# Rows of dV from TensorE products instead of DMA transposes, with other work moved between the stages of an attention segment

## The chip, the cores and the metric

The kernel runs on one NeuronCore of a Trainium2 chip. A core has five instruction streams: TensorE (PE: matrix products; PEld are its weight loads), VectorE (DVE), ScalarE (ACT), GpSimd (POOL) and SyncE (SP), which only starts DMAs. Products are written to PSUM[...]. The metric is the time of one execution on the device in microseconds; lower is better.

## The reference

A forward pass and all its gradients in one program. Segments of 32 tokens with 8 memory rows each run one after the other, since the memory of a segment is the first 8 output rows of the one before; the gradient runs through the same chain backwards. There are 64 segments, 32 heads of 128, a model width of 512 and a GLU of width 1792.

```python
for s in range(n_seg):
    xs = x[:, s * seg_len:(s + 1) * seg_len, :].copy()
    h = jnp.concatenate([mem, xs], axis=1)
    q = jnp.einsum('btd,dhe->bhte', h, Wq)
    k = jnp.einsum('btd,dhe->bhte', h, Wk)
    v = jnp.einsum('btd,dhe->bhte', h, Wv)
    scores = jnp.einsum('bhqe,bhke->bhqk', q, k) * scale
    scores = jnp.where(mask[None, None], scores, -1000000000.0)
    p = _softmax(scores, axis=-1)
    o = jnp.einsum('bhqk,bhke->bhqe', p, v)
    o = jnp.einsum('bhte,hed->btd', o, Wo)
    mem = o[:, :M, :].copy()
    outs.append(o[:, M:, :])
...
h = _layernorm(x, axis=-1) * (1 + ca) + sa
x = x + ga * _A_ref(h, A_mem0, A_Wq, A_Wk, A_Wv, A_Wo, A_seg_len)
h = _layernorm(x, axis=-1) * (1 + cb) + sb
x = x + gb * _B_ref(h, B_w_gate, B_w_up, B_w_down)
...
_out, _vjp = jax.vjp(_f, A_x, A_mem0, A_Wq, A_Wk, A_Wv, A_Wo, B_w_gate, B_w_up, B_w_down, c, w_mod)
```

The six parts `sa, ca, ga, sb, cb, gb` are the rows of `silu(c) @ w_mod`; the program returns the output and the eleven gradients.

## The kernel before, in words

The program has four stages: the forward segments (`phase2`), the GLU with its own gradients (`phase3`), the backward segments (`phase4`), and the weight gradients of the attention with the last layer-norm gradients (`phase5`, lines 1757 to 1831).

**Tiles.** The 32 heads of a segment are packed three to a group: eleven groups, each a 128-wide block in which three heads have 40 rows each. A tile of 1408 columns holds all eleven groups. Work on it is cut into three parts of four, four and three groups, each one PSUM bank (`pi` = 0, 1, 2). A product with the 32 rows of a segment as stationary operand uses only 32 columns of TensorE's array; four such products stand side by side by `tile_position`, and make one PSUM tile of 128 partitions that has to be summed over its four blocks afterwards ("fold"). `col_pass` (line 241) projects the rows of a segment this way, `col_mm` (209) and `pair_mm` (215) sum over heads; `pair_mm` uses two blocks for one half of the 512 columns and two for the other, so that its result is 256 wide.

**Tails.** The last 8 tokens of each segment do not depend on the chain (only the first 8 rows feed it), and neither do their gradients. Those rows are collected for four segments (`TailRows`, 1869) and multiplied once for all four, in pieces that `chunk()` puts where the caller wants them. In the same way `proj_b`/`turn_b` make the tail rows of q, k, v (forward) or of dO (backward) for the next four segments. `s4` is the place of a segment in its group of four; forward it runs 0 to 3, backward 3 to 0.

**A forward segment** (656 to 857): projections k, q, v (16 products for each half), whose rows `RA` are moved by VectorE and ScalarE; transposes of k and q (`turns`); scores and exponent (`st_exp`, 685), with one product of the identity and the mask added in PSUM for each of the eleven groups (691); a shift of v rows (`vshift`, 718); denominators (`den`, 697) in a tile of their own; weighted sums (`pv`); reciprocal and scaling (`ost`); transposes of the scaled rows (`ott`, 749); output projection in pairs; split of the result in a high and a low bf16 part (`split_pair`, 223), and the fold (`sum_pair`, 232), in which for each of four column blocks one product takes the high and one the low part. ScalarE copies the first 8 rows into the next segment's `hT` (841). The layer-norm of later tokens runs in between in steps `p1(j, 1..4)` (386 to 415): step k of a group stands in segment `s4` = k between the k and the q projection (766), the last before `ott(0)`. In segments 8 to 23 eight products of one part of `w_mod` stand between the denominators of parts 0 and 1 (805 to 810). PSUM: seven banks in one ring (`psp`) and one for tails.

**A backward segment** (1457 to 1610): the dO pass (`col_pass` with `WoT`, both halves moved as 512 columns to `RAd`, by VectorE and ScalarE), copies of `RAd` to `dOst` on GpSimd (1538), transposes of `RAd` (`turn`, 1384) moved to `dOT`, then `gv0` (dVT part 0), `dp` (11 products), `gv1`, `ds` (11), the sum over heads with `WvT`, transposes of dS (`dstt`), dKT and dQT (`grad_mm`, 1504), sums with `WkT`, the rest of `WvT`, and `WqT`, all in one tile `dh_ps`; `fold_split` (298) into four 256-wide pieces, one `chunk()` of 24 tail products while that goes on, `fold_sum` (313) with eight products, and the first 8 rows as `dyT` for the next segment. Behind the fold stand `proj_b` (16 products) in the segments `s4` = 3 and 2, and `turn_b` in 1.

The weight gradients need dV, dK and dQ with tokens in the partitions. `grad_out` (1513) has the transposed tile: after its last part SP starts a DMA transpose into `rows_x` (1517), and GpSimd later stores the rows (`row_stores`, 1519). Two wait for the next segment, behind its dO pass (`store_rows_x(1)`, 1541), the third until line 1567. GpSimd also starts the DMAs that bring the tail rows of dO into `dOst` (`dO_tails`, 1440). The tail gradients of a group come in by `get_da`/`get_db` in `s4` = 3 (1463, 1566). PSUM: six banks in a ring, one for `dh_ps`, one for tails.

`pin` (278) fixes each engine's order in both segment loops as it is written.

Of the kernel before, what the change touches and what calls it, by code (L numbers as in the profile page):

```python
# [40 lines left out]
class K:  # L41
# [146 lines left out]
    def mod_rest(self, psp, pool, k):  # L188
# [3 lines left out]
        st = {}  # L192
# [5 lines left out]
        def products():  # L198
# [4 lines left out]
            row = pool.tile([1, 128], F32, name="modrow", bufs=1)  # L203
            nc.scalar.activation(row[:], ps[0:1, :], AF.Copy)
            nc.gpsimd.dma_start(self.MODROW[:, sl], row[:])
# [26 lines left out]
    def sum_pair(self, psp, parts, name, tag):  # L232

        ft = psp.tile([128, self.cfg.DC, 32], F32, name=name + "_ft", tag=tag)
        for c in range(self.cfg.DC):
            for i in range(2):
                self.nc.tensor.matmul(ft[:, c, :], lhsT=parts[i][:, (c % 2) * 128:(c % 2) * 128 + 128],
                                      rhs=self.foldhalf[:, c // 2, :], start=(i == 0), stop=(i == 1))
        return ft

    def col_pass(self, psp, w, hf, lhs, rows, eng):

        E, DC = self.cfg.E, self.cfg.DC
        ps = psp.tile([128, 512], F32, name="pass_ps", tag="p")
        for c in range(DC):
            wc = w[:, c, :].rearrange("p (h e) -> p h e", e=E)
            for j in range(4):
                rhs = wc[:, 12 * hf + j:12 * hf + j + 10:3, :] if j < 3 else wc[:, 24 + 4 * hf:28 + 4 * hf, :]
# [4 lines left out]
        self.evac(eng, rows[:, 512 * hf:512 * hf + 512], ps[:])  # L253
# [44 lines left out]
    def fold_split(self, pool, ps, name, tags=""):  # L298

        nc = self.nc  # L300
        parts = []
        for h in range(2):
            sl = slice(256 * h, 256 * h + 256)
            hi = pool.tile([128, 256], BF16, name=name + "_hi", tag=f"{tags}hi{h}", bufs=1)
            nc.scalar.activation(hi[:], ps[:, sl], AF.Copy)  # L305
            parts.append(hi)
        for h in range(2):
            lo = pool.tile([128, 256], BF16, name=name + "_lo", tag=f"{tags}lo{h}", bufs=1)
            nc.vector.tensor_tensor(lo[:], ps[:, 256 * h:256 * h + 256], parts[h][:], op=ALU.subtract)  # L309
            parts.append(lo)  # L310
        return parts

    def fold_sum(self, psp, parts, name, tag):

        ft = psp.tile([128, self.cfg.DC, 32], F32, name=name + "_ft", tag=tag)
        for c in range(self.cfg.DC):
            for i in range(2):
                self.nc.tensor.matmul(ft[:, c, :], lhsT=parts[2 * i + c // 2][:, (c % 2) * 128:(c % 2) * 128 + 128],  # L318
                                      rhs=self.foldsel[:], start=(i == 0), stop=(i == 1))
# [109 lines left out]
    def phase2(self):  # L429
# [13 lines left out]
        with ExitStack() as ctx:  # L443
# [212 lines left out]
            for s in range(NS):  # L656
# [148 lines left out]
                if mod_r:  # L805
                    mod_r.pop()()
# [1213 lines left out]
```

## Time and profile before

| | |
|---|---|
| median of 4 runs | 3157.77 us (3151.9 to 3168.25) |
| profiled execution, its own time | 3168.25 us |
| its span, first to last instruction | 3166.4 us |
| mean granted TensorE clock | 0.985 |
| busy: TensorE / VectorE / GpSimd / ScalarE | 2985.0 / 1611.1 / 1481.0 / 1161.3 us |
| matmuls | 40069 |

The same by stretches of the span, in microseconds of busy time:

| stretch | us | TensorE | VectorE | ScalarE | GpSimd | DMA share |
|---|---|---|---|---|---|---|
| 50 to 1010, forward segments | 960 | 927.0 | 605.2 | 467.4 | 626.1 | 0.85 |
| 1010 to 1380, GLU | 370 | 327.9 | 263.0 | 132.0 | 199.0 | 0.87 |
| 1380 to 1580, its weight gradients | 200 | 190.4 | 56.3 | 41.5 | 35.5 | 0.76 |
| 1580 to 2590, backward segments | 1010 | 947.7 | 518.4 | 447.7 | 452.2 | 1.10 |
| 2590 to 3166, weight gradients | 576 | 568.9 | 144.0 | 64.0 | 158.7 | 0.67 |

A line of the profile names the source line, the engine, the operation, the tile written and those read, the shape, and either a start and a length (timeline) or sums. A wait line reads: who waited, for whom, microseconds in total, times, the longest. The end of a matmul is modelled[...], so the start of the next product is the better mark of what one costs.

### The profile page before, as it was taken

The numbers are of one execution on the slowest core, as the hardware profiler recorded it, in microseconds if no ns is written. First come the engines' busy times: TensorE is split into PE (matmuls) and PEld (weight loads), VectorE is DVE, ScalarE is ACT, GpSimd is POOL, SyncE is SP. The second block draws the span as 40 slices with busy tenths as digits, with TensorE's granted clock in tenths as the row PEclk, the third lists the DMA queues.
The fourth block names the chain that finished last, engine by engine and source line by source line (L and its number), as shares of the span: only waits on it lengthen the run. The fifth ranks groups of instructions, "written<-read, shape, count | busy, mean of one in ns | idle before, by whom it ended". The sixth has DMA issues, their size and how long they took to land.

```text
span 3166.4 us, 98844 instructions
## 1 busy us (share of the span) xinstructions
PE 2985.0 (94%) x40069; PEld 1730.3 (55%) x40069; DVE 1611.1 (51%) x3770; ACT 1161.3 (37%) x2829; POOL 1481.0 (47%) x2974
## 2 busy tenths in 40 slices
PE   5999999999998799989989999999899999999999
PEld 3666666666665444445555555555555554455454
DVE  4666666666655677742245555555455442222321
ACT  2444454445444333322144444444444430000111
POOL 3666666666665466531244444444344432233322
PEclk8999999999999899999999999999999999999999
DMA  8888788988888799898599999999999998666664
GB/s 292 206 206 210 193 207 201 202 200 210 200 205 238 174 218 211 215 273 263 195 227 263 267 254 259 264 276 266 238 256 261 242 286 298 212 196 215 196 231 145
DMA packets 936796, 726.14 MB, mean 229 GB/s; under 512 B 635954, under 2 KB 808530, under 8 KB 935956
## 3 DMA queue, kind: packets, MB, share of 16 engines
q1 hardware_dynamic: 806564, 509.77, 68.9%
q0 software_dynamic: 59120, 148.64, 13.8%
q10 hardware_dynamic: 70656, 61.41, 6.2%
q8 instruction: 316, 5.18, 0.7%
q14 instruction: 140, 1.15, 0.1%
HBM read 294.93 MB, written 276.35 MB: 180 GB/s over the span
## 4 chain that ended last, share of the span: by engine, by line
PE 44%; DMA 5%; issue 4%; ACT 2%; POOL 1%; DVE 1%; SPq 0%; ACTq 0%; POOLq 0%; DVEq 0%
PE dh_ps L212 10%; PE gps L1812 8%; PE pass_ps L249 4%; PE gps5o L1826 4%; PE g_ps L1509 3%; PE gps L1210 3%; PE dh_tps L212 2%; PE tps L1423 2%; PE dp_ps L1488 1%; DMA dOst<-RBd 1%; PE dp_ps L1496 1%; ACT RAd L61 1%; PE dh_ft L318 1%; POOL out_dram L1816 1%; PE turn_ps L1389 1%
## 5 line engine op out<-in xcount | busy, mean ns | idle before, releaser
L1812 PE MATMUL gps<-rows,hrows 128*128 128x512 bf16 (+2 forms) x2160 | 417.5, 355 | 0.0
L1812 PEld LDWEIGHTS <-hrows 128*128 128x128 bf16 x2160 | 211.1, 98 | 204.7
L249 PEld LDWEIGHTS <-hT 128*32 128x32 bf16 x6144 | 158.1, 97 | 161.5 <-issue 1.9
L1538 POOL COPY dOst<-RAd 96x512 bf16<-96x512 bf16 x128 | 78.3, 612 | 353.5 <-DVE RAd L63 342.2
L851 POOL TENSOR_TENSOR Pst<-Pst,rden 120x1408 bf16<-120x1408 bf16 x63 | 160.1, 2542 | 106.1 <-issue 77.9
L1816 POOL DMA_DIRECT2D out_dram<-ot x108 | 81.5, 755 | 253.9 <-DVE ot L63 138.5
L63 DVE CAST ot<-gps 128x512 bf16<-128x512 f32 (+3 forms) x76 | 48.1, 633 | 279.1 <-PE gps L1812 193.0
L61 ACT ACTIVATE ot<-gps 128x512 bf16<-128x512 f32 (+3 forms) x75 | 41.3, 551 | 353.9 <-PE gps L1812 211.2
L309 DVE TENSOR_TENSOR dh_lo<-dh_ps,dh_hi 128x256 bf16<-128x256 f32 x128 | 48.4, 420 | 240.3 <-ACT dh_hi L305 240.3
L212 PE MATMUL dh_ps<-WvT,dVT 128*32 128x512 bf16 x2048 | 136.3, 386 | 0.1
L1498 DVE SCALAR_TENSOR_TENSOR dS<-dp_ps,Pst_l 128x512 bf16<-128x512 f32 (+1 forms) x192 | 112.2, 640 | 44.0 <-PE dp_ps L1496 43.9
L249 PE MATMUL pass_ps<-Wv,hT 128*32 128x512 bf16 x2048 | 133.3, 380 | 0.0
L1826 PE MATMUL gps5o<-WoT,rows 128*128 128x512 bf16 x592 | 128.4, 379 | 1.1 <-DMA rows<-OSR 1.1
L249 PE MATMUL pass_ps<-WoT,dyT 128*32 128x512 bf16 x2048 | 123.6, 384 | 5.2 <-ACT dyT L1597 5.2
L220 PE MATMUL at_ps<-Wo,OT 128*32 128x256 bf16 x4096 | 125.3, 275 | 0.5 <-DVE OT L63 0.2
L249 PE MATMUL pass_ps<-Wk,hT 128*32 128x512 bf16 x2048 | 123.3, 383 | 1.5 <-ACT hT L841 1.1
L61 ACT ACTIVATE dVT<-g_ps 128x512 bf16<-128x512 f32 (+1 forms) x192 | 107.8, 561 | 44.7 <-PE g_ps L1509 28.6
L212 PE MATMUL dh_ps<-WkT,dKT 128*32 128x512 bf16 x2048 | 122.3, 380 | 0.0
L212 PE MATMUL dh_ps<-WqT,dQT 128*32 128x512 bf16 x2048 | 122.1, 379 | 0.0
L249 PE MATMUL pass_ps<-Wq,hT 128*32 128x512 bf16 x2048 | 121.6, 379 | 0.0
L63 DVE CAST RA0v<-pass_ps 128x512 bf16<-128x512 f32 x128 | 88.3, 690 | 64.8 <-PE pass_ps L249 62.3
L693 ACT ACTIVATE ET<-st_ps 128x480 bf16<-128x480 f32 (+1 forms) x192 | 96.1, 535 | 54.0 <-ACT qT L61 37.1
(413 smaller groups left out, 7072.1 us busy)
## 6 DMA issues: line engine op xcount, KB each, us to landing
OSR<-Ost SPq DMA_DIRECT2D x64, 352.0 KB
OT<-OT SPq DMA_DIRECT2D x64, 352.0 KB
VT<-VTr SPq DMA_DIRECT2D x64, 352.0 KB
PS<-Pst SPq DMA_DIRECT2D x64, 352.0 KB
OT_l<-OT SPq DMA_DIRECT2D x64, 352.0 KB
Pst_l<-PS SPq DMA_DIRECT2D x64, 352.0 KB
VT_l<-VT SPq DMA_DIRECT2D x64, 352.0 KB
DKR<-rows_x POOLq DMA_DIRECT2D x64, 352.0 KB, 5.6
```

The costliest lines, as they stand in the source:

```text
L61: return nc.scalar.activation(out, in_, AF.Copy)
L63: return nc.vector.tensor_copy(out, in_)
L212: self.nc.tensor.matmul(ps[32 * j:32 * j + 32, :], lhsT=lhsT, rhs=w, start=(n < 4), stop=(n >= total - 4), tile_position=(0, 32 * j))
L220: nc.tensor.matmul(ps[32 * j:32 * j + 32, :], lhsT=x[k], rhs=w[k][:, 256 * d:256 * d + 256], start=(n == 0), stop=(n == total - 1), tile_p ...
L249: self.nc.tensor.matmul(ps[32 * j:32 * j + 32, :], lhsT=lhs(c), rhs=rhs, start=(c == 0), stop=(c == DC - 1), tile_position=(0, 32 * j))
L693: nc.scalar.activation(part3(ET, pi)[:, 0:n, 0:120], st_ps[:, 0:n, 0:120], AF.Exp, scale=cfg.scale)
L851: nc.gpsimd.tensor_tensor(Pst[0:120, :, :], Pst[0:120, :, :], rden[:, :].unsqueeze(2).to_broadcast([120, G, 128]), op=ALU.mult)
L1210: nc.tensor.matmul(ps[:], lhsT=h2r[:, j, c * 128:(c + 1) * 128], rhs=xr[:, j, :], start=(j == 0), stop=(j == NT - 1))
L1498: nc.vector.scalar_tensor_tensor(out=part3(dS, pi), in0=ps[:, 0:n, :], scalar=cfg.scale, in1=part3(Pst, pi), op0=ALU.mult, op1=ALU.mult)
L1812: nc.tensor.matmul(ps[:, 0:ng * E], lhsT=hrows[:, tp_, c * 128:(c + 1) * 128], rhs=rows[:, tp_, 0:ng * E], start=(tp_ == 0), stop=(tp_ == ...
L1816: nc.gpsimd.dma_start(outw[c * 128:(c + 1) * 128, h0:h0 + 3 * (ng - 1) + 1:3, :], ot[:, 0:ng * E].rearrange("p (h e) -> p h e", e=E))
L1826: nc.tensor.matmul(pss[gg][:], lhsT=src[0][:, src[1], gg * E:(gg + 1) * E], rhs=dyrows[:, tp_, :], start=(tp_ == order[0]), stop=(tp_ == o ...
```

## The change

Five things, all in the two segment loops.

1. *Rows of dV.* The DMA transpose of dVT is gone. `rv(pi, eng)` computes the rows directly: the same product with its operands exchanged, eleven more products in a segment, moved to `rows_x` by ScalarE, ScalarE and VectorE. dK and dQ keep their DMA transposes.
2. *dO pass.* Its second half is cut into two quarters, each moved as 256 columns by ScalarE. Between pass and turn stands other work: half of a `proj_b` half (8 products) after the segments `s4` = 0 and 3, a tail piece of 8 in `s4` = 1 and 0. The tail pieces are seven, of 16, 24, 8, 8, 16, 8, 16 products, instead of four of 24.
3. *Fold.* The dQ part is summed in pairs in a tile of its own (`dht_pairs`). dV and dK are split as whole 512-wide tiles, into `dST`, while the dQ products run; only the 256-wide pair is split after them. `fold_sum` has 16 products in place of eight.
4. *Queues.* The stores of dV and dK rows stand at the end of the segment, ahead of the fold, in place of behind the next dO pass; the load of Kst stands ahead of the dQT transpose; `get_da`/`get_db` come a segment earlier.
5. *Forward.* The mask is written to PSUM a segment ahead, by three products of 480, 480 and 360 columns between the `ott` transposes; the score tiles get three banks of their own, the ring five. The denominators go into the free block of the third `pv` tile. The layer-norm steps 1 to 3 move behind the output projection, the products of `w_mod` to segments 4, 7, 8, 12 and on in fours to 60, ahead of `ott(0)`. `ott` parts are moved by ScalarE, VectorE, ScalarE instead of VectorE, ScalarE, VectorE. The forward fold takes both high parts' products ahead of the low ones.

The diff, cut to its core:

```diff
 def sum_pair(self, psp, parts, name, tag):
-        for c in range(self.cfg.DC):
-            for i in range(2):
+        for i in range(2):
+            for c in range(self.cfg.DC):
...
 def fold_split / fold_sum:
+        hi, lo = (pool.tile([128, 512], BF16, name=f"{name}_{x}", tag=x, bufs=1)[:, :] if home is None
+                  else home[:, 512 * i:512 * i + 512] for i, x in enumerate(("hi", "lo")))
+        nc.scalar.activation(hi, ps[:], AF.Copy)
+        nc.vector.tensor_tensor(lo, ps[:], hi, op=ALU.subtract)
...
+        mms = [(t[:, c * 128:(c + 1) * 128], self.foldsel[:], c) for t in parts for c in cs]
+        mms += [(t[:, (c % 2) * 128:(c % 2) * 128 + 128], self.foldhalf[:, c // 2, :], c) for t in pair for c in cs]
...
 phase2:
-            psp = ctx.enter_context(tc.tile_pool(name="p2ps", bufs=7, space=PSUM))
-            psb = ctx.enter_context(tc.tile_pool(name="p2psb", bufs=1, space=PSUM))
+            psp = ctx.enter_context(tc.tile_pool(name="p2ps", bufs=5, space=PSUM))
+            pst = ctx.enter_context(tc.tile_pool(name="p2pst", bufs=3, space=PSUM))
...
+            def mask_mm(pi):
+                n = min(PG, G - pi * PG)
+                ps = masked[pi] = pst.tile([128, PG, GW], F32, name="st_ps", tag="st")
+                nc.tensor.matmul(ps[:, 0:n, 0:120], lhsT=self.ident[:, :], rhs=maskT[:, 0:n, :], start=True, stop=False,
+                                 skip_group_check=True)
...
-                        nc.tensor.matmul(st_ps[:, j, 0:120], lhsT=self.ident[:, :], rhs=maskT[:, :], start=False, stop=True)
...
-                if 1 <= s4 <= 3:
-                    p1(s // nseg_t + P1_AHEAD, s4)
...
+                turned = bool(slots.get((s4, "turn"))) or bool(mod_r)
+                mod_row = mod_r.pop()() if mod_r else None
...
+                if more and not turned:
+                    mask_mm(more.pop(0))
+                    mask_mm(more.pop(0))
                 ott(0)
+                if len(more) > 1:
+                    mask_mm(more.pop(0))
                 ott(1)
+                if len(more) > 1:
+                    mask_mm(more.pop(0))
                 ott(2)
+                if more:
+                    mask_mm(more.pop(0))
...
                 evac_turned()
+                if mod_row:
+                    mod_row()
+                if s4 < 3:
+                    p1(s // nseg_t + P1_AHEAD, s4 + 1)
...
 phase4:
+            tail = TailRows(self, sb2, psp, psb, 3, "dh", self.DHB, (16, 24, 8, 8, 16, 8, 16), home=dSs[0])
...
+                def rv(pi, eng):
+                    n = min(PG, G - pi * PG)
+                    self.evac(eng, rv_rows[:, pi * PG:pi * PG + n, :], grad_mm("dV", Pst, dOst, pi)[:, 0:n, :])
+                    if pi == NP - 1:
+                        dram = self.DVR[s]
+                        row_stores.insert(0, lambda: nc.gpsimd.dma_start(dram, rv_rows[:]))
...
+                for a, n, eng in ((0, 4, "dve"), (4, 2, "act"), (6, 2, "act")):
+                    self.col_pass(psp, WoT, 0, lambda c: dyT[:, c, :], RAd, eng, steps=(a, n))
                 for hf in range(2):
-                    self.col_pass(psp, WoT, hf, lambda c: dyT[:, c, :], RAd, ("dve", "act")[hf])
                     nc.gpsimd.tensor_copy(dOst[0:96, 512 * hf:512 * hf + 512], RAd[0:96, 512 * hf:512 * hf + 512])
-                if pend:
-                    pend.pop()()
-                store_rows_x(1)
+                b_done = b_rest.pop()() if b_rest else None
+                if s4 < 2:
+                    tail.chunk()
...
                 dht(dVT, WvT, 1)
+                rv(0, "act")
...
+                grad_out("dVT", dVT, 2, "act", gv2)
+                for pi in range(NP):
+                    grad_out("dKT", dKT, pi, "dve", gks[pi])
+                    if pi == 1:
+                        rv(1, "act")
+                rv(2, "dve")
...
                 dht(dVT, WvT, 2)
+                parts = self.fold_split(sb2, dh_ps[0], "dh", dST)
+                pair = self.split_pair(sb2, dht_pairs(dQT, WqT), "dh")
+                tail.collect(s % nseg_t, [dVT, dKT, dQT])
+                tail.chunk()
                 if split:
                     self.pop_later()
-                for pi in range(NP):
-                    dht(dQT, WqT, pi)
...
+                store_rows_x(1)
+                ft = self.fold_sum(psp, parts, "dh", "p", pair)
...
+                elif s4 == 3 and g > 0:
+                    b_rest.append(proj_b(g - 1, 1, 2))
+                elif s4 == 2:
+                    tail.chunk()
+                elif s4 == 1 and g > 0:
+                    turn_b(g - 1)()
+                elif s4 == 0 and g > 1:
+                    b_rest.append(proj_b(g - 2, 0, 2))
```

`proj_b(t, hf, parts)` now takes a tile from the bank of `dh_ps`, does the first of its parts and returns a function for the rest.

## The prediction

> **What bounds the kernel now.** I read the busy shares, then the table of stretches, then TensorE's waits, then the timelines of TensorE and VectorE inside one segment. The page gives TensorE 94% of the span; VectorE has 51%, GpSimd 47%, ScalarE 37%. The stretches show where the change acts: the 64 forward segments fill about 50 to 1010 us, the 64 backward ones about 1580 to 2590. Columns: microseconds and instruction counts for TensorE, its weight loads, VectorE, ScalarE, GpSimd; then TensorE's clock, DMA share, GB/s.
>
> ```profile
> 50.00:1010.00 960.00, 926.95 (x17772) 597.44 (x17762) 605.23 (x1475) 467.41 (x1269) 626.08 (x1336) 1.00 0.85 203
> ...
> 1580.00:2590.00 1010.00, 947.65 (x15851) 570.64 (x15847) 518.42 (x1368) 447.67 (x1147) 452.16 (x1113) 0.99 1.10 258
> ```
>
> Both stages are TensorE queues in program order, and the backward one loads the DMA engines to 1.10 (transfers overlap). TensorE's named waits are small:
>
> ```profile
> PE turn_ps L1389 <- ACT RAd L61: 24.5, 64, 0.6
> PE g_ps L1509 <- DMA dOst<-RBd: 16.5, 5, 6.1
> ...
> PE tps L715 <- DVE Ost L744: 10.0, 34, 0.3
> ```
>
> They understate the loss: a short gap hides in the modelled ends of the matmuls. The distance between two starts is the real price. In a backward segment (columns: start, length, instruction, and in brackets the idle time and its releaser):
>
> ```profile
> 2097.26 1.90 PE L249 MATMUL pass_ps<-WoT,dyT 128*32 128x512 bf16 x32
> 2099.17 0.40 PE L1389 MATMUL turn_ps<-ident,RAd 128*128 128x128 bf16 x4
> 2099.93 0.40 PE L1389 MATMUL turn_ps<-ident,RAd 128*128 128x128 bf16 x4 [0.36 <-ACT RAd L61]
> 2100.16 0.39 PE L1509 MATMUL g_ps<-Pst_l,dOst 128*128 128x128 bf16 x4
> 2100.39 0.87 PE L1488 MATMUL dp_ps<-VT_l,dOT 128*128 128x128 bf16 x11
> 2101.09 0.39 PE L1509 MATMUL g_ps<-Pst_l,dOst 128*128 128x128 bf16 x4
> ...
> 2105.12 1.01 PE L1509 MATMUL g_ps<-dST,Kst 128*128 128x128 bf16 x11
> 2106.07 1.91 PE L212 MATMUL dh_ps<-WkT,dKT 128*32 128x512 bf16 x32
> ...
> 2109.96 0.60 PE L212 MATMUL dh_tps<-WvT,dh_tail 128*32 128x512 bf16 x8
> ```
>
> The 32 products of the dO pass take 1.74 us (54.4 ns each), eleven 128-wide products 0.62 (56 ns), both from undisturbed stretches of this timeline. The dO pass starts at 2097.26 and the second dVT group at 2101.09: 3.83 us for 1.74 + 8 x 0.056 + 4 x 0.056 + 11 x 0.056 = 3.03 us of work, so 0.80 is lost around the turn. The dQT group takes 0.95 for 0.62. The first turns of the segments lie regularly 16.05, 15.47, 14.76 and 14.80 us apart (61.08 for a group of four). From the first (1580.53) to the last (2575.97) are 995.4; 63/4 x 61.08 is 962.0. Of the other 33.4 us, 7.3 are in the first segment and 26 in hiccups such as this one:
>
> ```profile
> 2285.61 0.40 PE L1389 MATMUL turn_ps<-ident,RAd 128*128 128x128 bf16 x4 [0.36 <-ACT RAd L61]
> 2289.82 0.78 PE L1509 MATMUL g_ps<-Pst_l,dOst 128*128 128x128 bf16 x4 [3.81 <-DMA dOst<-RBd]
> 2290.39 1.38 PE L1488 MATMUL dp_ps<-VT_l,dOT 128*128 128x128 bf16 x11
> ```
>
> The tail DMA of dO came late, and after it eleven products take 1.17 us instead of 0.70 to 0.77: the hiccup is paid twice. In the forward segment TensorE ends the last weighted sum at 550.58 and waits 0.45 for the scaled rows:
>
> ```profile
> 549.86 0.38 PE L732 MATMUL or_ps<-Vst,ET 128*128 128x128 bf16 x4
> 550.30 0.21 PE L703 MATMUL dc_ps<-ones,ET 128*128 128x1 bf16 x3
> 550.41 0.33 PE L732 MATMUL or_ps<-Vst,ET 128*128 128x128 bf16 x3
> 551.03 1.09 PE L715 MATMUL tps<-ident,Ost 128*128 128x128 bf16 x11 [0.29 <-DVE Ost L744]
> ...
> 552.30 1.93 PE L220 MATMUL at_ps<-Wo,OT 128*32 128x256 bf16 x64
> ```
>
> [...] 56 ns for 128 columns, and eight 32-column fold products take 0.2 us. So the three wide mask products cost what eleven narrow ones did. [...]
>
> **The change part by part**, against this execution (3168.25 us, span 3166.4).
>
> Backward, per segment, offsets from the start of the dO pass.
> - *dO pass.* Its second half is evacuated in two 256-wide pieces (381 ns, the row of dh_hi) and eight 512-wide products (0.44 us) of tail or RB work are put before the turn. The pass ends at 1.74; ScalarE starts 0.28 after an end (2099.0 to 2099.28), so the last piece is there at 2.40 and the second turn at 2.45. Then ScalarE and VectorE must move four dOT pieces of about 0.45 (two each), and the dp products wait for them some 0.25 and 0.19. Second dVT group at 3.95 instead of 3.83: +0.12 with 0.44 of work inside.
> - *dV rows.* Eleven products, 0.62. Their three tiles rotate through the same six banks, so the dQT tiles now wait for the second and third dKT evacuation: VectorE is done with dST at about 8.3 (7.48 today, 2104.74, plus the 0.8 that the transposes come later) and needs 0.58 for each, TensorE asks at 9.2 and 9.7 and is served 0.2 and 0.3 later; it lost 0.33 there before. Sum +0.80. ScalarE gets 2 x 0.56 more and VectorE 0.55, beside TensorE's 1.74 us of dK.
> - *Fold.* dV and dK are split beside the dQ pairs (64 x 27.5 ns = 1.76, the rate of the forward output projection), only 256 columns remain. Eight more fold products cost 0.2. Pairs' end to fold's end was 1.83 with 24 tail products; with 16 it is 0.87 + 0.40 = 1.27, with 24 (one segment of four) 1.71.
> - *After the fold.* 0.97, 0.97, 0.55, 0.47 before (16, 16 products, a turn, nothing); now eight products or a turn in each, about 0.5, which just covers ScalarE's dyT.
> - Group of four: 4 x 0.12 + 4 x 0.80 - 3 x 0.56 - 0.12 - 0.96 = +0.92; 16 groups: **+15 us**. Bounds: +52 if the 19 added products (0.82 x 64) come without less waiting; -41 if the waits of 0.44 at dp and about 0.45 at dQT vanish too.
> - *DMA.* One transpose of three goes; its 352 KB row store stays. SP needs 1.4 to 8.0 us to issue one dVT transpose, and in the hiccup it was this one that took 7.95. The Kst load moves ahead of the dQT transpose, daq one segment earlier. I take **-20** of the 26 us of hiccups; bounds 0 and -26.
>
> Forward.
> - *Masks.* The score products shrink from 1.15 to 0.57 us, but the chain does not follow: the V shift waits for RA0v, which VectorE ends 0.88 after the scores start (548.08 + 0.69 against 547.89), so the second denominators come at 1.69 instead of 1.87 and the scaled rows about 0.17 earlier. Of the 0.55 us of masks most fills the 0.45 gap and the gaps between the output transposes. Net about 0.1: **-6 us**; bounds 0 and -28 (0.45 x 63).
> - *Layer-norm steps.* Today they stand between the k and q evacuations:
>
> ```profile
> 512.26 2.64 DVE L399 TENSOR_SCALAR xh<-x,mv,rstd 128x512 f32<-128x512 bf16 x1
> 514.94 0.69 DVE L400 TENSOR_TENSOR xh<-xh,ca_bc 128x512 f32<-128x512 f32 x1
> 515.55 0.68 DVE L63 CAST RA0q<-pass_ps 128x512 bf16<-128x512 f32 x1
> ```
>
>   RA0q comes 1.2 us late, TensorE's turn waits 0.68 at 516.29. The new place is VectorE's 1.84 us gap during the output projection. The 62 distances between score starts after the first (21.1) sum to 937.7; undisturbed groups (14.89, 14.75, 14.69, 14.79) would give 916, so 22 are lost; segments 8 to 23 with the modulation products sum to 249.8, segments 32 to 47 to 240.7, so 9 of the 22 are theirs. I take **-10** of 13 for the steps (0 if they delay at_lo instead) and **-7** of 9 for the products, which move into the gap.
> - *Fold order.* hi products first hide 0.1 of the 0.22 between hi and lo (about 60 segments): **-6**.
> - Seven banks become five plus three for scores: every fifth tile's reader is done before it is wanted in this timeline, the closest being V (546.80 against 546.91). Cost 0.
>
> Sum 15 - 20 - 6 - 10 - 7 - 6 = **-34 us**: 3134 for this execution, and 3157.77 - 34 = **3124** at the median, which is 10.5 below it.
>
> **Rivals.** *A: the fillers work wholly.* Also the waits at dp and the added one at dQT go, 0.64 x 63 = 40: 3084. For it: most of these evacuations are under 0.5 us and their engines are half idle. Against: their order is fixed. *B: only the place of the waiting changes.* Backward pays 52, DMA -20, forward -29: 3161. For it: the dQT banks. Against: 0.80 us of turn wait cannot outlive 0.44 us of other work wholly. *C, the slower side: GpSimd's queue.* The dV and dK row stores now stand at the segment's end, before the next segment's dOst copies; the dK store waits there for its transpose. GpSimd arrives about 11.7 after the dO pass begins (its last tail copy starts at 2108.62 today); the copies, 0.61 each, are due before the first dVT group of the next segment, at 15.35 + 2.68 - 0.61 = 17.4, and two stores of 0.56 stand ahead of them. The transpose is issued near 9.8 (2107.06 today), so a landing later than 6.5 us after its issue delays TensorE by the excess. Above 0.8 us per segment the kernel is slower; at 1 us, 3187. For it: SP took up to 3.8 us for a dKT transpose alone. Against: GpSimd waited only ten times (18.6 us) for these rows when it asked near 18.5, and a third of the transposes is gone.
>
> **How the numbers follow.** The sum 52%, its own range 3100 to 3147; A 20%, B 16%, C 12%. Range 3078 to 3165: from A's middle to just above B's; C and half of A's better side are left out. A measurement of this kernel tells about 0.5% (16 us) from no change, so faster means below 3142. Faster 0.52 x 0.93 + 0.20 = 0.68; same 0.18 (B, and the worse end of the sum); slower 0.14 (C, and B's end).
>
> **What would show it.** Turn-to-turn distances near 15.5 in every backward segment, not 16.05 to 14.76; no dOst wait over 1 us; DMA share near 0.95; TensorE's wait for ScalarE's RAd gone, waits at dp and dQT grown. Forward: score distances near 14.7 without 16 us ones. It is wrong if backward distances exceed 15.8 (B), if GpSimd waits for dKT rows in most segments (C), or if forward segments stay above 14.9.

## The result, and the profile after

The changed kernel takes 3154.85 us (median of 35 runs, 3140.96 to 3169.62) against 3163.39 for the kernel before (56 runs beside them): ratio 0.9974, 95% interval 0.9964 to 0.9983. It is faster by 8 us, where 34 were forecast. Its profiled execution took 3147.36 us (span 3145.5), the one of before 3168.25 (3166.4). Before's lies in the upper quarter of its runs (43rd of 56, from the fastest) and after's low among its own (6th of 35), so the pair shows 21 us where the medians show 8.

To place the time, I take three distances between starts on TensorE from each trace: over the forward stage (first to last output projection, 63 segments), from there to the first turn of the backward stage, and over the backward stage (first to last turn of RAd).

| trace | forward | between | backward | span |
|---|---|---|---|---|
| before | 954.0 | 566.9 | 995.4 | 3166.4 |
| after | 931.6 | 567.9 | 997.5 | 3145.5 |

So the forward stage gained 22.4 us, and the backward stage, where the relief of the DMA engines was to come, gained nothing. The table of stretches of the changed kernel (columns as in the prediction) shows the relief itself:

```profile
50.00:1010.00 960.00, 936.29 (x17503) 588.38 (x17503) 561.68 (x1423) 500.71 (x1335) 631.19 (x1345) 0.99 0.80 210
1580.00:2590.00 1010.00, 980.59 (x20024) 698.13 (x20016) 575.04 (x1418) 526.02 (x1305) 446.99 (x1098) 1.00 1.01 238
```

The backward stage's DMA share fell from 1.10 to 1.01, and TensorE is busy 33 us longer in those 1010 us. (The stage lies 22 us earlier in this trace. From first to last turn of each trace the shares are 1.11 and 1.00, and TensorE is busy 934 and 965 us.) TensorE's waits in the changed kernel (us in total, times, longest):

```profile
PE g_ps L1547 <- POOL dOst L1594: 22.3, 22, 3.4
...
PE g_ps L1547 <- DMA dOst<-RBd: 6.7, 1, 6.7
```

The 64 waits for ScalarE's RAd are gone, and only one wait for the DMA of dO's tails is left, in the first segment. In their place stands a wait that before did not have: 22 segments in which the dVT group waits for GpSimd's copy into dOst. What held GpSimd stands in the page's costliest groups (busy and mean ns, then idle time before and what ended most of it), and in its timeline at the worst of these places:

```profile
L1557 POOL DMA_DIRECT2D DKR<-rows_x x64 | 35.4, 553 | 283.6 <-DMA rows_x<-dKT 277.7
```

```profile
1606.11 0.56 POOL L1566 DMA_DIRECT2D DVR<-rows_x  x1
1614.54 0.56 POOL L1557 DMA_DIRECT2D DKR<-rows_x  x1 [7.87 <-DMA rows_x<-dKT]
1615.09 0.28 POOL L1392 COPY dyT<-daq 128x96 bf16<-128x96 bf16 x1
1615.29 1.17 POOL L1594 COPY dOst<-RAd 96x512 bf16<-96x512 bf16 x2
```

GpSimd issues the dV row store at 1606.11, then stands 7.87 us before the dK row store until the DMA transpose of dKT has landed, and only then, at 1615.29, copies RAd into dOst. TensorE's timeline at the same place:

```profile
1615.97 0.40 PE L1547 MATMUL g_ps<-Pst_l,dOst 128*128 128x128 bf16 x4 [3.42 <-POOL dOst L1594]
...
1617.21 1.33 PE L1534 MATMUL dp_ps<-negones,OT_l 128*128 128x128 bf16 x11
1618.33 0.31 PE L333 MATMUL dh_tp<-ident,dh_tb 128*128 128x128 bf16 x1
1618.57 2.49 PE L216 MATMUL dh_ps<-WvT,dVT 128*32 128x512 bf16 x24
```

It waits 3.42 us, and then the 24 dV products take 2.49 us instead of the 1.48 of other segments and the eleven before them 1.33 instead of 0.78. That is 3.4 + 1.6, and this segment's turn-to-turn distance is 20.17 instead of 15.09. The trace's record of the granted clock stands at 0.5 of full speed for 3.41 us from 1617.25. It does so from 1866.42 too, where a wait of 2.04 us ends, and stays at full speed after two waits of 2.4 us (2116.65 and 2478.39). In the trace of before it stands at 0.5 for 6.83 us from 2288.52, in the last 1.3 us of the wait of 3.81 us that the prediction shows and for 5.5 us after it. At all three places the products are slower; what decides whether a wait brings half the clock is not shown here.

Away from such places the backward segments are regular: 15.29, 15.75, 15.12 and 15.09 us, 61.25 for a group of four against 61.08 before. 63/4 x 61.25 is 964.7; the distance of 997.5 holds 7.9 us more in the first segment and 25 us of hiccups, as many as the 26 of before. The 22.3 us of waits for dOst and the two stretches at half clock (an estimate: up to half of 3.41 us lost in each) make up these 25.

In the forward stage the gap before the output transposes is filled, as the timeline shows:

```profile
546.40 0.77 PE L742 MATMUL or_ps<-Vst,ET 128*128 128x128 bf16 x7
547.01 0.22 PE L713 MATMUL or_ps<-ones,ET 128*128 128x1 bf16 x3
547.08 0.56 PE L656 MATMUL st_ps<-maskT,ident 128*128 128x480 bf16 x2
547.57 1.02 PE L725 MATMUL tps<-ident,Ost 128*128 128x128 bf16 x11
548.43 0.32 PE L656 MATMUL st_ps<-maskT,ident 128*128 128x360 bf16 x1
...
548.79 1.38 PE L224 MATMUL at_ps<-Wo,OT 128*32 128x256 bf16 x44
```

The wide masks stand at 547.08 where TensorE waited 0.45 us for the scaled rows, and the regular segments lie 14.59, 14.70, 14.93 and 15.04 us apart; the 15.4 to 16.7 of segments 8 to 23 are gone. Such a group of four, 59.26 us, is no shorter than the undisturbed ones of before (59.12 by the prediction's figures): the forward gain is that the longer segments are gone.

### The profile page after: what moved, and what is told of

The parts are those of the page before. It is cut to its first block, busy times and chain, and to the rows that moved or that the text cites. A ratio compares the mean times of both kernels' runs of the same rounds, so it can differ in the third digit from the quotient of the medians.

```text
span 3145.5 us, 106217 instructions
## 1 busy us (share of the span) xinstructions
PE 3009.2 (96%) x43845; PEld 1840.9 (59%) x43845; DVE 1618.3 (51%) x3738; ACT 1272.5 (40%) x3053; POOL 1480.2 (47%) x2974
## 3 DMA queue, kind: packets, MB, share of 16 engines
q14 instruction: 140, 1.15, 0.1%
## 4 chain that ended last, share of the span: by engine, by line
PE 42%; DMA 7%; issue 5%; POOL 2%; DVE 1%; ACT 0%; SPq 0%; POOLq 0%; ACTq 0%; DVEq 0%
PE gps L1883 9%; PE dh_ps L216 6%; PE g_ps L1547 5%; DMA rows_x<-dKT 5%; PE gps5o L1897 4%; PE pass_ps L256 3%; PE gps L1234 3%; PE dhq_ps L224 3%; PE dh_tps L216 2%; PE dp_ps L1526 1%; PE tps L1459 1%; PE dp_ps L1534 1%; POOL out_dram L1887 1%; PE turn_ps L1413 1%; DVE dKT L63 1%
## 5 line engine op out<-in xcount | busy, mean ns | idle before, releaser
L1557 POOL DMA_DIRECT2D DKR<-rows_x x64 | 35.4, 553 | 283.6 <-DMA rows_x<-dKT 277.7
L256 PE MATMUL pass_ps<-WoT,dyT 128*32 128x256 bf16 (+1 forms) x3072 | 122.5, 308 | 0.9 <-ACT dyT L1663 0.9
L224 PE MATMUL dhq_ps<-WqT,dQT 128*32 128x256 bf16 x4096 | 122.9, 273 | 0.0
L336 POOL DMA_DIRECT2D DHA<-dh_rb x64 | 34.8, 544 | 179.5 <-PE g_ps L1547 158.2
L224 PEld LDWEIGHTS <-dQT 128*32 128x32 bf16 x4096 | 109.6, 97 | 15.9
```

What stands on the lines that cost most here:

```text
L224: nc.tensor.matmul(ps[32 * j:32 * j + 32, :], lhsT=x[k], rhs=w[k][:, 256 * d:256 * d + 256], start=(n == 0), stop=(n == total - 1), tile_p ...
L256: self.nc.tensor.matmul(ps[32 * j:32 * j + 32, :], lhsT=lhs(c), rhs=rhs, start=(c == 0), stop=(c == DC - 1), tile_position=(0, 32 * j))
```

## The experiments

The theory at this point (Q): the change freed the DMA engines and TensorE as meant, but moved the dK row store ahead of the next segment's dOst copies on GpSimd, and the wait of that store for its transpose costs what the freed transposes gave. The rival (D): the DMA engines are full, somebody always waits for them, and the name of the waiting instruction says little.

**e1: both row stores behind the dOst copies again.** Where the dV buffer is taken in the text had to move for it. By the traces, this moves nothing on VectorE, ScalarE or SyncE in the segment loops, and on GpSimd only the stores.

```diff
                     nc.gpsimd.tensor_copy(dOst[0:96, 512 * hf:512 * hf + 512], RAd[0:96, 512 * hf:512 * hf + 512])
+                store_rows_x(1)
                 b_done = b_rest.pop()() if b_rest else None
...
-                store_rows_x(1)
                 ft = self.fold_sum(psp, parts, "dh", "p", pair)
```

> The changed kernel, but the dV and dK row stores go back behind the next segment's dOst copies on GpSimd, where the kernel before had them; nothing else is undone. Theory Q (GpSimd's queue: a store that waits for the dK transpose holds up the dOst copies, TensorE waits about 1 us in 22 segments and runs slower after it): TensorE's wait for dOst of L1594 (22.3 us, 22 times) falls below 3 us, the backward turn-to-turn distance from first to last falls from 997.5 by 15 to 25 us, the kernel takes about 3135 us (ratio to before 0.990 to 0.993). Theory D (the DMA engines are full, whoever waits for them): the wait returns under another name, dOst<-RBd or rows_x, the distance stays within 6 us of 997.5, the time within 5 us of the changed kernel's 3155.

Measured: 3201.92 us, ratio 1.0123 (1.0105 to 1.014), backward distance 1043.9. Neither theory had this: D had named rows_x as a place where the wait may come back, but with an unchanged distance. The wait for dOst of L1594 did vanish (0.2 us, once), but another came; first TensorE's waits of this run, then ScalarE's:

```profile
PE g_ps L1547 <- ACT rows_x L61: 54.6, 48, 5.6
...
PE g_ps L1547 <- POOL dOst L1596: 0.2, 1, 0.2
```

```profile
ACT rows_x L61 <- DMA DVR<-rows_x: 118.2, 38, 7.4
```

dV's rows are now written by ScalarE into one of three row buffers, and in this order the store of the previous segment's dV rows is issued only after the dO pass, so that the buffer is still being read when ScalarE wants it. ScalarE waits 118 us (110.7 of them inside the stage), and TensorE behind it. The run says nothing for or against Q; it says that the dV store must be early, for a reason that did not exist when the rows came from a DMA.

**e2 and e3: each half of the change alone** (the other stage's functions are those of the kernel before, with the helpers that they call).

> The forward half of the change alone: the backward stage is the one of the kernel before, word for word. Theory F (the traces are right: the forward stage gains 22 us, the backward one nothing): about 3141 us, ratio 0.993, and the forward distance 931 to 934 us. Rival G (the forward gain is partly an accident of the one profiled run): 3150 to 3157, ratio 0.996 to 0.998, or a forward distance above 940.

> The backward half of the change alone: the forward stage is the one of the kernel before, word for word. Theory F: as before or slightly slower, 3160 to 3172 us, ratio 0.999 to 1.003, backward turn-to-turn distance 995 to 1005, with the waits for dOst of L1594 in it. Rival G: faster by 5 us or more, ratio below 0.9985.

Measured: forward half alone 3147.39 us, 0.9944 (0.9926 to 0.9961), forward distance 931.7. Backward half alone 3173.58 us, 1.0042 (1.0025 to 1.006), backward distance 994.6, with 18.1 us of waiting for dOst copies in 18 segments. The forward gain holds in every trace (930.8 to 932.1 where the forward half is the changed one); e2's ratio makes it 12 to 23 us. The backward half makes the kernel slower by 8 to 19 us. Theory F had it right in kind and too mild in size: the one trace of before and of after made the backward half look free. Where the backward half loses these 8 to 19 us is not shown: e3's own distance, 994.6, is that of before (995.4, and 998.3 in e2, which has before's backward stage). Its trace is longer only between the stages, by 6 us, where traces of one kernel differ by as much (see e4).

**e4: the changed kernel again**, for a second trace.

> The changed kernel itself, once more, on the same chip as the runs beside it, for a second trace. If the 12 us between the profiled pair (3168.25 and 3147.36) and the medians (3163.4 and 3154.9) are the luck of the two profiled runs: about 3155 us again, forward distance within 3 us of 931.6, and a backward distance that differs by some us from 997.5 because the hiccups lie elsewhere. If the forward distance moves by more than 5 us, the forward gain itself is not steady.

Measured: 3158.55 us, 0.9977 (0.9959 to 0.9996); the profiled run's span 3164.7. Forward distance 931.5, backward 1006.5 (22 waits for dOst copies, 27.6 us), and the part between them, which the change hardly touches, 576.8 instead of 567.9. So one pair of profiles can be out by 9 us in that part alone (566.9 to 578.0 over the fourteen traces of this study), and by as much again where the hiccups fall differently.

**e5: only the dK row store behind the copies, the dV store stays early.**

```diff
+                store_rows_x(1)
                 b_done = b_rest.pop()() if b_rest else None
...
-                store_rows_x(1)
+                store_rows_x(2)
                 ft = self.fold_sum(psp, parts, "dh", "p", pair)
```

> The changed kernel, but only the dK row store goes behind the next segment's dOst copies; the dV store stays at the segment's end, so that ScalarE's first dV row evacuation finds its buffer free (in e1 it waited 110.7 us for the dV store). Theory Q (GpSimd's wait for the dK transpose is what costs the backward stage its gain): TensorE's wait for dOst of L1594 falls from 22 to 28 us to below 5, the backward turn-to-turn distance from 997 to 1006 down to 975 to 987, the time to 3132 to 3145 us (ratio 0.990 to 0.994). Theory R (three row buffers are too few: the dK transpose now waits for the late dK store, and the hiccup only moves): the distance stays between 993 and 1008, the time between 3150 and 3162, and SP's transposes wait for DKR<-rows_x in most segments.

Measured: **3126.64 us, 0.9902 (0.9884 to 0.992)**, faster than both kernels. Backward distance 972.9. TensorE's waits on the gradient groups are down to the one of the first segment:

```profile
PE g_ps L1547 <- DMA dOst<-RBd: 6.8, 1, 6.8
```

GpSimd's timeline in a segment of this run:

```profile
2069.30 0.56 POOL L1568 DMA_DIRECT2D DVR<-rows_x  x1
2069.85 0.28 POOL L1392 COPY dyT<-daq 128x96 bf16<-128x96 bf16 x1
2075.29 1.17 POOL L1596 COPY dOst<-RAd 96x512 bf16<-96x512 bf16 x2 [5.16 <-DVE RAd L63]
2076.41 0.55 POOL L1557 DMA_DIRECT2D DKR<-rows_x  x1
```

The dOst copies start as soon as VectorE delivers RAd, and GpSimd then issues the dK store without any wait. The 62 turn-to-turn distances after the first lie between 14.58 and 15.78; of 25 us of hiccups none is left (972.9 - 964.7 = 8.2, and the first segment alone is 9.4 us longer than its like). In the segment loops the traces of e5 and of the changed kernel have the same order on VectorE, ScalarE and SyncE, and on GpSimd only this store has moved: one store put behind the copies is worth 0.7% of the kernel. Q is shown, and theory R is not: SP's transposes wait 30.5 us in all for DKR<-rows_x, and TensorE does not notice.

**e6: dV rows by DMA transpose again**, the eleven products left out, stores where before had them, the rest of the change kept.

```diff
-                    if pi == NP - 1 and nm != "dVT":
+                    if pi == NP - 1:
...
-                rv(0, "act")
...
-                    if pi == 1:
-                        rv(1, "act")
-                rv(2, "dve")
```

> The changed kernel with the rows of dV computed by DMA transposes of dVT again, and the dV and dK row stores behind the next segment's dOst copies as in the kernel before; the eleven products a segment are left out, fold, fillers and forward stay changed. Theory T (the eleven products are paid in full, the transposes cost little): regular groups of four near 59 us (61.25 less up to 4 x 0.62), the backward distance 970 to 990, about 3130 to 3145 us. Theory D (three transposes a segment are what makes the hiccups): the DMA share returns to about 1.1, waits for dOst<-RBd of several us come back, and the distance is 995 or more, the time 3152 or more.

Measured: 3163.09 us, 1.0014 (0.9997 to 1.0031), backward distance 990.0. Its stretch, and TensorE's longest waits in the backward stage ("issue" is a wait for which the profile names nothing):

```profile
1580.00:2590.00 1010.00, 950.57 (x19512) 669.48 (x19512) 538.41 (x1359) 473.42 (x1190) 448.12 (x1107) 0.98 1.15 261
```

```profile
PE g_ps L1547 <- DMA dOst<-RBd: 34.0, 16, 6.2
PE pass_ps L256 <- issue: 14.5, 14, 2.1
PE turn_ps L1413 <- issue: 6.0, 3, 3.2
```

The regular group of four is 58.07 us (14.48, 15.01, 14.30, 14.28) instead of 61.25: the products cost 0.80 us a segment, the value forecast. But the DMA share is 1.15, dO's tails land 6.8 us after their issue in the median instead of 5.0 in e5, 16 segments wait for them, and the distance holds 990.0 - 914.6 = 75 us beyond its groups, 8 of them in the first segment. Of the other 67, 28 are waits for dO's tails and 24 are "issue" waits, of which the changed kernel and e5 have none over 0.3 us; for the rest, the trace's clock stands at 0.5 for 27 us in these segments. What the "issue" waits are is open. So the rows on TensorE cost 0.80 x 63 = 50 us of products and remove 67 us of hiccups: a gain of 17 in the distance (990.0 to 972.9), provided that GpSimd's order lets it through. (The two times differ by more, 36 us; in the two spans, 29 us apart, the other 12 lie outside the backward stage.) The two theories share the result: the groups are T's, and the distance lies at the upper end of T's range, while the DMA share, the waits and the time are D's. D is right about three transposes, and wrong about two.

**e7 and e8: two forward terms undone**, on the changed kernel. e7 puts the masks back beside their scores; e8 the layer-norm steps back between the k and q evacuations.

In e7:

```diff
+                    mask_mm(pi)
                     st_ps = masked.pop(pi)
...
-                more = list(range(NP)) if s + 1 < NS else []
+                more = []
```

In e8:

```diff
+                if 1 <= s4 <= 3:
+                    p1(s // nseg_t + P1_AHEAD, s4)
                 proj("q", 0, "dve")
...
-                if s4 < 3:
-                    p1(s // nseg_t + P1_AHEAD, s4 + 1)
```

> The changed kernel with the mask products back in front of their score products, in the same three banks and still three wide ones a segment; the rest stays. The prediction's step (masks worth 6 us): forward distance 931.6 + 6 = 937 or 938, time 3158 to 3162. If the masks fill real gaps (bound 28): distance 950 to 960. If the regular group, 59.26 us against 59.1 before, tells right that they are worth nothing: distance within 2 us of 931.6, time as the changed kernel's.

> The changed kernel with the layer-norm steps of the tiles ahead back in their old place, between the k and the q projection's evacuations; the rest stays. The prediction's step (worth 10, at most 13): forward distance 941 to 945, time 3165 to 3168. If the steps are behind most of the measured 22: distance 948 to 953, time 3171 to 3176. If they were worth nothing and the modulation products and masks made the gain: within 3 us of 931.6.

Measured: forward distance 936.0 (e7; 937 or 938 by the prediction's step) and 935.1 (e8) against 931.6, so 4.4 us for the masks and 3.5 for the layer-norm steps. The times, 3151.47 us (0.9977, 0.9967 to 0.9987) and 3150.89 (0.998, 0.9967 to 0.9994), cannot tell: their runs spread over 20 and 37 us by the hiccups of the backward stage. None of the three values given for e8 was right; the nearest, "worth nothing", was 0.5 us off its bound.

**e9 and e10: the other two forward terms undone**, on e5, whose runs spread over 6 us only. e9 puts the modulation products back into segments 8 to 23, between the weighted sums and evacuated at once; e10 the fold of the output projection back to hi and lo in turn.

In e9:

```diff
-                if s + 1 in mod_at:
+                if mod_r:
+                    mod_r.pop()()()
+                if 8 <= s < 8 + 4 * DC:
```

In e10:

```diff
-        for i in range(2):
-            for c in range(self.cfg.DC):
+        for c in range(self.cfg.DC):
+            for i in range(2):
```

> From here on the base is e5 (dK store behind the copies; ratio 0.9902, forward distance 930.8, backward 972.9), because its runs spread over 6 us only. This run is e5 with the modulation products in segments 8 to 23 again, and each between the weighted sums with its row evacuated at once, as in the kernel before. Prediction's step (the products are worth 7 to 9 us): forward distance 938 to 940. What is left over of the measured 22 after masks (4.4) and layer-norm steps (3.6) is 14: if it is all theirs, 943 to 946. If the remainder comes from elsewhere in the segment: within 3 us of 930.8.

> e5 with the fold of the forward output projection in its old order, hi and lo in turn for each of the four column blocks. Prediction's step (0.1 us in some 60 segments): forward distance 937, time 6 us above e5's. Rival (TensorE reaches the lo products late either way, since VectorE's subtraction follows ScalarE's copy): within 1.5 us of 930.8.

Measured: e9 forward distance 936.3 (938 to 940 by the prediction's step), 3128.93 us, 0.9898 (0.9876 to 0.9921); e10 936.3 (937), 3133.45 us, 0.9909 (0.9885 to 0.9933). So 5.5 us for each against e5's 930.8. The ratios of e9 to e12 all lie inside e5's interval, so these runs are read by their distances. In e9 fifteen of the sixteen segments with products lie at 15.24 to 15.59 and one at 15.87; they are 0.65 longer than their like (the last 0.94), while the fourth segment of every other group falls from 15.04 to 14.73: at the old place the products cost 0.65 us a segment, at the new one 0.31, so that half of their price is still paid. The four terms undone one at a time sum to 4.4 + 3.5 + 5.5 + 5.5 = 19 of the 22.4 us. The first of the 63 distances varies by itself, from 14.47 to 15.42 in the eight traces with the changed forward half, while the other 62 sum to 916.3 to 916.7 in all of them. By these 62 the terms are 3.7, 3.1, 5.5 and 4.8, together 17 of 21. What the rest comes from was not tried.

**e11: the products before the turn put ahead of the dO pass**, on e5; the quarter-wide evacuations stay.

```diff
+                b_done = b_rest.pop()() if b_rest else None
+                if s4 < 2:
+                    tail.chunk()
                 for a, n, eng in ((0, 4, "dve"), (4, 2, "act"), (6, 2, "act")):
...
-                b_done = b_rest.pop()() if b_rest else None
-                if s4 < 2:
-                    tail.chunk()
```

> e5 with the eight to sixteen products that stand between the dO pass and its turn put ahead of the pass instead; the same work, another place. If they are what covers ScalarE's last evacuation of RAd (the prediction's step): the wait turn_ps<-RAd comes back at 0.3 to 0.6 us in each segment that has such products, the backward distance grows by 15 to 35 us over 972.9. If the two quarter-wide evacuations alone had made the wait short: the distance grows by less than 8 us.

Measured: 3134.42 us, 0.9917 (0.9892 to 0.9942), backward distance 978.6, 5.7 us above e5 (e9 and e10, with e5's backward stage, have 973.2 and 974.6). TensorE's timeline without anything between pass and turn:

```profile
2075.76 0.61 PE L256 MATMUL pass_ps<-WoT,dyT 128*32 128x256 bf16 x16
2076.36 0.78 PE L1413 MATMUL turn_ps<-ident,RAd 128*128 128x128 bf16 x8
2077.07 0.38 PE L1547 MATMUL g_ps<-Pst_l,dOst 128*128 128x128 bf16 x4
2077.29 0.78 PE L1526 MATMUL dp_ps<-VT_l,dOT 128*128 128x128 bf16 x11
2077.90 0.39 PE L1547 MATMUL g_ps<-Pst_l,dOst 128*128 128x128 bf16 x4
```

The eight transposes of the turn take 0.71 us to the next start instead of 0.46 in the changed kernel; no wait turn_ps<-RAd is listed in the whole run. The narrow evacuations had made the turn nearly ready by themselves; the products between cover 0.1 us a segment.

**e12: dV rows by DMA in one segment of four**, on e5.

```diff
-                    if pi == NP - 1 and nm != "dVT":
+                    if pi == NP - 1 and (nm != "dVT" or s4 == 2):
...
-                rv(0, "act")
+                if s4 != 2:
+                    rv(0, "act")
```

> e5 with the dV rows of one segment in four (the second of each group in time) by DMA transpose, so that its eleven products are left out. In e6 the products were worth 0.80 us a segment and three transposes everywhere brought some 69 us of hiccups. If the DMA engines have room for a quarter of them: backward distance about 972.9 less 16 x 0.8 = 960, the time about 3114 us (ratio 0.986). If not: hiccups of over 13 us in all, distance 970 or more, ratio 0.990 or more.

Measured: 3131.64 us, 0.991 (0.9881 to 0.9938), distance 972.2: no gain. The segments without the products are 0.75 shorter (15.00), and the next ones mostly 15.4 to 16.6 instead of 15.12. GpSimd's waits, then TensorE's:

```profile
POOL DVR L1557 <- DMA rows_x<-dVT: 79.9, 16, 6.1
...
POOL DKR L1557 <- DMA rows_x<-dKT: 24.9, 14, 4.5
```

```profile
PE g_ps L1547 <- POOL dOst L1596: 7.9, 11, 1.5
```

Here the early dV store waits for a transpose, and the fault of the changed kernel is back in a smaller size. So the run doesn't tell whether the DMA engines have room for a quarter of the transposes: a dV store behind the copies in these segments was not tried.

## Why the prediction was wrong

The direction was right and the size was not. By the prediction's own steps, us, each against the distance that it speaks of:

| step | forecast | measured | from |
|---|---|---|---|
| backward, regular groups | +15 | +3 (16 x 0.17) | groups 61.25 against 61.08 |
| DMA hiccups | -20 | -1 (+7 in e4) | 25 (33) us against 26 |
| masks | -6 | -4.4 (-3.7 without the first distance) | e7 |
| layer-norm steps | -10 | -3.5 (-3.1) | e8 |
| modulation products | -7 | -5.5 (-5.5) | e9 |
| fold order | -6 | -5.5 (-4.8) | e10 |

**The step that failed is "DMA": "I take -20 of the 26 us of hiccups".** It counted what the change takes off the DMA engines and not what it does to GpSimd's queue. The first half was right: with two transposes, dO's tails no longer come late after the first segment (one wait is left, 6.7 us), and e5, which differs in the place of one store, has lost every hiccup, more than the 20. The second half was in the prediction as rival C, and the mechanism is C's to the letter: the dK store waits for its transpose, ahead of the next segment's dOst copies. (The timeline above shows it: the copies of RAd start at 1615.29, behind a store that stood 7.87 us for rows that they do not use.) The prediction had even worked out the edge: a landing later than 6.5 us after the issue of the dKT transpose. Measured from that issue to the dK store on GpSimd, which starts as the rows land, the changed kernel's segments show 5.5 to 10.2 us, 7.0 in the median, 40 of 64 above 6.5 (e4: 46 of 64, median 7.2). Not every one of these is felt, but 22 segments are, by 1 us in the mean, with slower products behind two of the waits. C was weighed only as "slower", at 12%; that it could be about as large as the saving had no place among the cases, and the likeliest case charged nothing for it.

**Regular groups.** The dV rows cost 0.81 us a segment by the starts (0.80 forecast, e6 the same). The mis-sized term is the dO pass: forecast +0.12 a segment, measured 3.79 from the start of the pass to the second dVT group in the median against 3.90, -0.11. The changed kernel, which this timeline shows:

```profile
2080.29 1.91 PE L256 MATMUL pass_ps<-WoT,dyT 128*32 128x512 bf16 x48
2082.03 0.60 PE L256 MATMUL pass_ps<-WoT,dyb 128*32 128x512 bf16 x8
2082.56 0.62 PE L1413 MATMUL turn_ps<-ident,RAd 128*128 128x128 bf16 x8
2083.02 0.39 PE L1547 MATMUL g_ps<-Pst_l,dOst 128*128 128x128 bf16 x4
2083.27 0.96 PE L1526 MATMUL dp_ps<-VT_l,dOT 128*128 128x128 bf16 x11
2084.06 0.39 PE L1547 MATMUL g_ps<-Pst_l,dOst 128*128 128x128 bf16 x4
```

The pass begins at 2080.29, the filler at 2082.03, the turn at 2082.56, and the second dVT group at 2084.06: 3.77. The forecast had this turn's second half at 2.45 and the dp products waiting 0.44 behind it; the eleven dp products take 0.79 to the next start instead of 0.62, so that wait was 0.17. The 0.23 x 64 = 15 us are more than the 12 between +15 and +3; by difference, the fold and the products after it gave some 3 us less than forecast. The wait at dQT was read from one segment: 0.95 us for the group there, but 0.71 in the median of the 64 segments before, and 0.76 after. The forecast's reason for a turn without wait, 0.44 us of other work inside, was also mostly wrong: e11 shows that the narrow evacuations did it.

**Forward.** Masks, modulation products and fold order came within 2.3 us of their terms. That three wide mask products cost what eleven narrow ones did is shown: by the starts 0.56 us in the changed kernel (203, 203 and 153 ns in the median) and 0.58 before (11 x 53 ns). The layer-norm term was too large by 6.5 to 7: the prediction took the 13 us that were lost outside the modulation segments as theirs, but in the changed kernel, put back in their old place, the steps lengthen 11 of the 48 segments that have them, by 0.1 to 0.6 us, and not the others. Whether they cost more beside the other old parts was not tried.

**The remainder** is the yardstick. The sum was made against one execution, 3168.25 us, and set down from there to the median of four, 10.5 us below. The medians of the runs made since (3158.6 to 3164.6 for the kernel before) are 1 to 7 us above that median, and the change itself is worth 8.5 by the medians. The terms of the traces, 3 - 1 - 22 = -20 and 3 + 7 - 22 = -12, go beyond it by 4 to 12 us; the part between the stages varies by 11 by itself, so that two traces cannot settle it closer.

Of "what would show it", the RAd wait is gone, and so are the forward segments of 16 us (two of the four regular ones, 14.93 and 15.04, are above the 14.9 that would tell against it). The DMA share fell to 1.01, not to 0.95. Backward segments near 15.5 came only away from the hiccups. "No dOst wait over 1 us" did not come: after the first segment the DMA of dO's tails no longer holds TensorE, but GpSimd's copies do, for up to 3.4 us. The waits at dp and dQT hardly grew (the dp group takes 0.77 us to the next start in the median before and after). What the prediction named as C's mark, GpSimd waiting for dKT rows in most segments, came as well: 62 times, 277.7 us.

## What to carry to other kernels

GpSimd's queue, in program order, passed the wait of one store on to the copies behind it (7.87 us at the place shown): before a store is moved forward, ask what its own input waits for, and what stands behind it on that engine; "it stands earlier" is not "it is done earlier". When a transfer is turned into computed rows, its buffer rule turns round as well (e1): a destination that a DMA filled late is now wanted early by an engine, which waited 118 us for it in all. And a stage whose runs spread over 29 us (3140.96 to 3169.62) hides a change of 5; read such a change from distances between starts within the stage, or remove the hiccups first: e5's five runs spread over 6 us.

## What was not expected of the hardware

Three transposes a segment go with 26 us of hiccups while TensorE takes 61.08 us for a group (DMA share 1.10), and with 67 when it takes 58.07 (share 1.15): most of what TensorE saved came back, 28 us of it as waits for the DMA of dO's tails and 24 as waits for which the profile names nothing. A row store of 0.56 us on GpSimd's queue cost TensorE up to 3.9 us at once (e4) when it stood ahead of the copies, and nothing (e5) behind them. A wait of 2.04 us went with half the clock for 3.41 us, and two of 2.4 us did not. The part between the two stages, where the change alters next to nothing, took between 566.9 and 578.0 us, and 567.9 and 576.8 in two executions of the changed kernel itself.
